# Replacing the framework's instruction order by a kernel's own list schedule, in a fused sparse-attention and feed-forward kernel

## The chip, the cores and the metric

The kernel runs on one core of a Trainium2 chip. The metric is the device time of one execution in microseconds (us), as the median over several runs. Engines are named as the profile names them: PE is TensorE, DVE is VectorE, ACT is ScalarE, POOL is GpSimd, SP is SyncE, whose queue issues most of the DMAs.

## The reference

The reference is attention over selected chunks of 32 keys, followed by a feed-forward layer with a gate.

```python
q, k, v: (4, 8, 768, 64) float32            # batches, heads, positions, head size
k_min, k_max = min and max of k over each chunk of 32 positions
ub    = sum(maximum(q * k_min, q * k_max), -1)       # bound for each (position, chunk)
ub    = where(chunk is not in the future, ub, -1e9)
top   = the 6 chunks with the largest ub
mask  = (the key's chunk is in top) & (key position <= query position)
attn  = softmax(where(mask, q @ k.T / 8, -1e9))
x     = (attn @ v), heads side by side               # 3072 x 512
out   = (relu(x @ w_gate) * (x @ w_val)) @ w_out     # 512 -> 1536 -> 512
```

## The kernel before

The kernel walks through 20 jobs. A job is two heads of one batch; in batch 0 each pair of heads is cut into two jobs of 384 positions, so there are 8 small jobs and then 12 full ones. For each job it loads q, k and v, casts them to bf16 on POOL, transposes q and k, takes minima and maxima of k on DVE, computes bounds and the selection, writes the selection as extra rows of the operand `qx`, computes scores and exponentials, masks the diagonal blocks on POOL, multiplies by v, and transposes the result into `xT`. The feed-forward layer of a batch can start when all four jobs of its positions are done. It has units (a gate group and a value group of four matmuls each, then a relu on ACT and a product on DVE) and output tiles (12 matmuls, a copy on ACT, a store).

In batches 0 and 1 the transposes are done by PE; in batches 2 and 3 the DMA does them. That is so in both kernels.

```python
PE_KQ = PE_SEL = PE_X = lambda b: b < 2

def setup_rest():
    for kx in kx_l:                      # indicator rows: which key lies in which chunk
        for h in range(2):
            g = 64 - 64 * h
            nc.vector.tensor_scalar(out=kx[h][g:g + 64, :]..., in0=ident[...].to_broadcast(...),
                                    scalar1=DROP, scalar2=None, op0=ALU.mult)      # 64x768, eight of them
    # ... cut: memsets

def stage_SELT(j):                       # selection -> rows of qx
    sT = turned(st["sel"][:, ra:r1], r1 - ra, "sel", on_pe)
    eng = (nc.scalar, nc.vector) if on_pe else (nc.vector, nc.vector)
    halves([qx[1][0:64, ts], qx[0][64:128, ts]], sT, eng)
# ... cut: k and q copies in stage_TR choose their engines in the same way

def u_s1(b, nt, u, wide):                # one feed-forward unit
    # ... cut: two PSUM buffers, one each for gate and value (one double one if wide)
    for ps, w in ((g_ps, wg_sb[gi]), (v_ps, wv_sb[gi])):
        for kt in range(KT_):
            nc.tensor.matmul(ps, w[:, kt, cs], xTb[:, kt, x0:x0 + SH], ...)
    nc.scalar.activation(out=grl, in_=g_ps, func=ACT.Relu)
    nc.vector.tensor_tensor(out=hTb[:, nt, :], in0=v_ps, in1=grl, op=ALU.mult)

W_AT = {2: [(w_in, 0)], 4: [(w_in, 1)], 5: [(w_in, 2)], 6: [(w_in, 3)], ...}   # weights, issued by POOL

for s in range(-1, NJ + 2):              # order of recording; the framework's scheduler then
    stage_LD(s + 3); stage_CAST(s + 2)   # orders every engine by its own costs
    stage_UB(s + 1); stage_SELT(s + 1); stage_CASTV(s + 1); weights of W_AT[s + 1]
    stage_TR(s + 2)
    # ... cut: scores of s and attention-times-v of s - 1 alternate, with a quota of units
    stage_XT(s - 1)
```

The softmax here doesn't subtract the row's maximum and nothing guards it: scores larger than these inputs give would overflow.

## Time and profile before

| | before |
|---|---|
| median | 341.52 us (341.18 to 342.4, 4 runs) |
| span of the profiled run | 339.6 us |
| PE busy | 286.9 us (84%) |
| DVE, ACT, POOL busy | 197.9, 168.5, 90.3 us |

PE's busy time contains pipeline fill and half-speed stretches, so I use a second measure. Both kernels issue the same 2344 matmuls. Taking each at its columns / 2.4 GHz + 2.5 ns, and at least 27 ns (the matmuls of 48 columns start 25 to 29 ns apart once PE is at full speed), gives 258.0 us of streaming for the whole program. This is an estimate of the least time that PE needs; "lost" below is the time of a stretch less the streaming of the matmuls that start in it, so it holds idle time and the extra time of matmuls at half speed alike. The Trainium skill ("TensorE: Matmul & The Clock Gate", part 1) gives N / 2.4 GHz plus about 2.5 ns for a warm array: in the tail 22 units of 8 matmuls of 384 columns took 1.32 us each, against 1.30 by the formula. The program before loses 339.6 - 258.0 = 81.6 us.

From the page of the kernel before: busy times, then rows in which each digit is one fortieth of the span (8.5 us) in tenths busy, the granted PE clock, and the DMA engines; at last the small k loads, with the median time from issue to landing.

```profile
PE 286.9 (84%) x2318; PEld 170.7 (50%) x2344; DVE 197.9 (58%) x621; ACT 168.5 (50%) x269; POOL 90.3 (27%) x176
...
PE   1435578999788899987898979998999999999995
...
DVE  8953765888879994688876733354653310343300
...
PEclk9999999999989999997999999999999999999999
DMA  6999999999399794574541232221111023000022
...
k_raw<-in_k_dram SPq DMA_DIRECT2D x16, 96.0 KB, 5.0
```

PE climbs slowly for 60 us. DVE is near full in the first two slices. The DMA engines are full from the second slice to about 85 us.

From PE's list of waits (total us, number, longest us):

```profile
PE v_ps L375 <- DVE hTb L379: 8.9, 12, 2.2
PE o_ps L335 <- POOL aT L316: 6.5, 4, 5.4
```

From POOL's timeline (start, duration, instruction, idle time before it and who ended it):

```profile
10.33 0.91 POOL L411 DMA_DIRECT2D wg_61<-in_moe_w_gate_dram  x1
...
22.35 0.53 POOL L185 CAST vb_81<-v_raw 128x384 bf16<-128x384 f32 x1 [3.20 <-DMA v_raw<-in_v_dram]
26.48 0.51 POOL L180 CAST k_bf<-k_raw 128x384 bf16<-128x384 f32 x1 [3.60 <-DMA k_raw<-in_k_dram]
26.93 0.74 POOL L412 DMA_DIRECT2D wv_67<-in_moe_w_val_dram  x1
27.68 1.12 POOL L316 TENSOR_SCALAR_AFFINE_SELECT aT<-aT 128x256 bf16<-128x256 bf16 x3
```

These lines belong together. The weight DMAs begin at 10.3 us, in front of loads that are needed sooner. The k load of the fourth job is late, so the cast at 26.48 us stands waiting, and behind it in POOL's queue stand the masks of 27.68 us, whose first inputs, ACT's exponentials, were ready at 17.5 us. PE waits 5.4 us for them. The Trainium skill (same page, "Architectural detail", on engine queue depths) calls the queues of ACT and DVE strict FIFO, and GpSimd's strict FIFO for each of its cores; the trace agrees: the masks start at 27.68 us, after the late cast and a weight issue.

Two neighbouring matmuls of 384 columns, from PE's timeline:

```profile
47.61 0.52 PE L375 MATMUL g_ps<-xTb,wg_61 128*128 128x384 bf16 x1
47.93 0.52 PE L375 MATMUL v_ps<-xTb,wv_65 128*128 128x384 bf16 x1
```

They start 0.32 us apart, which is 1.2 GHz. This lasts until 58 us; afterwards such matmuls start 0.16 us apart. The skill's page describes this as the clock gate: an array that is not busy enough runs at half speed. The page's granted clock reads 9 (full) throughout these 58 us, but that is no measurement: the trace's first clock record starts at 58.5 us, and a stretch without a record is shown as full. The later records are full except for two stretches of 3.4 us at half speed, from 92.6 and from 154.1 us.

### The profile page before, as it was taken

The numbers are of one execution on the slowest core, as the hardware profiler recorded it, in microseconds if no ns is written. First come the engines' busy times: TensorE is split into PE (matmuls) and PEld (weight loads), VectorE is DVE, ScalarE is ACT, GpSimd is POOL, SyncE is SP. The second block draws the span as 40 slices with busy tenths as digits, with TensorE's granted clock in tenths as the row PEclk, the third lists the DMA queues.
The fourth block names the chain that finished last, engine by engine and source line by source line (L and its number), as shares of the span: only waits on it lengthen the run. The fifth ranks groups of instructions, "written<-read, shape, count | busy, mean of one in ns | idle before, by whom it ended". The sixth has DMA issues, their size and how long they took to land.

```text
span 339.6 us, 6292 instructions
## 1 busy us (share of the span) xinstructions
PE 286.9 (84%) x2318; PEld 170.7 (50%) x2344; DVE 197.9 (58%) x621; ACT 168.5 (50%) x269; POOL 90.3 (27%) x176
## 2 busy tenths in 40 slices
PE   1435578999788899987898979998999999999995
PEld 0213355566455555554455645464666554555542
DVE  8953765888879994688876733354653310343300
ACT  2472365588775534485355544463656532334221
POOL 3637707332563421274201202030201100000000
PEclk9999999999989999997999999999999999999999
DMA  6999999999399794574541232221111023000022
GB/s 141 176 199 211 216 213 212 219 189 226 74 204 192 141 163 138 151 128 87 55 88 20 46 21 85 83 88 19 25 19 27 0 87 116 31 2 0 2 93 93
DMA packets 108958, 36.32 MB, mean 107 GB/s; under 512 B 100224, under 2 KB 105856, under 8 KB 108928
## 3 DMA queue, kind: packets, MB, share of 16 engines
q1 hardware_dynamic: 103104, 31.21, 45.2%
q0 software_dynamic: 5824, 4.72, 9.1%
q8 instruction: 18, 0.29, 0.4%
q14 instruction: 12, 0.10, 0.1%
HBM read 28.31 MB, written 6.29 MB: 102 GB/s over the span
## 4 chain that ended last, share of the span: by engine, by line
PE 55%; DMA 16%; DVE 15%; ACT 4%; issue 3%; SPq 3%; POOL 2%; POOLq 0%; ACTq 0%; DVEq 0%
PE y_ps L386 17%; PE v_ps L375 9%; PE gv_w L375 9%; PE g_ps L375 8%; PE sT L305 6%; DMA v_raw<-in_v_dram 5%; PE o_ps L335 4%; DMA k_raw<-in_k_dram 4%; DVE hTb L379 3%; SPq L144 3%; DMA sel_tr<-sel_76 3%; DMA k_tr<-k_bf 2%; DVE kmm L221 2%; ACT aT L309 2%; DVE kmm L222 1%
## 5 line engine op out<-in xcount | busy, mean ns | idle before, releaser
L309 ACT ACTIVATE aT<-sT 128x1024 bf16<-128x1024 f32 x96 | 85.0, 919 | 41.0 <-PE sT L305 20.1
L316 POOL TENSOR_SCALAR_AFFINE_SELECT aT<-aT 128x256 bf16<-128x256 bf16 x96 | 39.1, 422 | 111.5 <-ACT aT L309 111.5
L379 DVE TENSOR_TENSOR hTb<-v_ps,grl 128x384 bf16<-128x384 f32 x72 | 39.9, 554 | 30.1 <-PE v_ps L375 15.1
L378 ACT ACTIVATE grl<-g_ps 128x384 bf16<-128x384 f32 x72 | 35.2, 489 | 36.9 <-PE g_ps L375 27.8
L335 PEld LDWEIGHTS <-aT 128*128 128x128 bf16 x672 | 31.6, 102 | 22.2 <-POOL aT L316 7.5
L386 PEld LDWEIGHTS <-hTb 128*128 128x128 bf16 x288 | 27.1, 98 | 30.3
L390 ACT ACTIVATE y_sb<-y_ps 128x512 f32<-128x512 f32 x24 | 14.3, 597 | 48.2 <-PE y_ps L386 45.2
L340 DVE RECIPROCAL zr<-o_ps 128x6 f32<-128x6 f32 (+1 forms) x40 | 7.4, 186 | 39.3 <-PE o_ps L335 38.9
L379 DVE TENSOR_TENSOR hTb<-gv_w,grl 128x384 bf16<-128x384 f32 x24 | 13.4, 558 | 21.8 <-ACT grl L378 21.8
L378 ACT ACTIVATE grl<-gv_w 128x384 bf16<-128x384 f32 x24 | 11.8, 490 | 20.4 <-PE gv_w L375 20.4
L375 PE MATMUL v_ps<-xTb,wv_65 128*128 128x384 bf16 x72 | 17.7, 339 | 2.9 <-DVE hTb L379 2.6
L341 DVE TENSOR_TENSOR x_sb<-o_ps,zr 128x384 bf16<-128x384 f32 (+1 forms) x40 | 19.1, 476 | 1.2
L386 PE MATMUL y_ps<-wo_71,hTb 128*128 128x512 bf16 x72 | 19.5, 379 | 0.1
L386 PE MATMUL y_ps<-wo_72,hTb 128*128 128x512 bf16 x71 | 19.4, 379 | 0.1
L386 PE MATMUL y_ps<-wo_70,hTb 128*128 128x512 bf16 x71 | 19.2, 379 | 0.1
L180 POOL CAST k_bf<-k_raw 128x768 bf16<-128x768 f32 (+1 forms) x20 | 14.4, 720 | 16.8 <-DMA k_raw<-in_k_dram 7.5
L386 PE MATMUL y_ps<-wo_69,hTb 128*128 128x512 bf16 x64 | 18.4, 378 | 0.4
L375 PE MATMUL g_ps<-xTb,wg_61 128*128 128x384 bf16 x72 | 16.8, 338 | 0.7 <-DVE xTb L354 0.6
L375 PE MATMUL v_ps<-xTb,wv_68 128*128 128x384 bf16 x72 | 14.9, 325 | 2.8 <-DVE hTb L379 2.7
L375 PE MATMUL v_ps<-xTb,wv_67 128*128 128x384 bf16 x72 | 14.8, 325 | 2.5 <-DVE hTb L379 2.3
L180 POOL CAST q_bf<-q_raw 128x768 bf16<-128x768 f32 (+1 forms) x20 | 14.3, 714 | 9.1 <-issue 4.9
L375 PE MATMUL v_ps<-xTb,wv_66 128*128 128x384 bf16 x72 | 14.8, 325 | 1.4 <-DVE hTb L379 1.3
(229 smaller groups left out, 541.0 us busy)
## 6 DMA issues: line engine op xcount, KB each, us to landing
out_dram<-y_sb SPq DMA_DIRECT2D x24, 256.0 KB, 2.0
k_raw<-in_k_dram SPq DMA_DIRECT2D x12, 384.0 KB, 5.8
q_raw<-in_q_dram SPq DMA_DIRECT2D x12, 384.0 KB, 6.0
v_raw<-in_v_dram SPq DMA_DIRECT2D x12, 384.0 KB, 4.2
k_raw<-in_k_dram SPq DMA_DIRECT2D x16, 96.0 KB, 5.0
q_raw<-in_q_dram SPq DMA_DIRECT2D x16, 96.0 KB, 5.2
v_raw<-in_v_dram SPq DMA_DIRECT2D x16, 96.0 KB, 5.2
wg_61<-in_moe_w_gate_dram POOLq DMA_DIRECT2D x1, 384.0 KB, 6.6
```

Of the source, the lines that this page charges most:

```text
L144: nc.sync.dma_start(out=t[:, h], in_=s[h].rearrange("(r p) d -> p r d", p=128))
L180: nc.gpsimd.tensor_copy(out=t, in_=st[nm + "r"].rearrange("p h r d -> p r h d"))
L305: nc.tensor.matmul(sT[:, h, o:o + w], kx[h][:, c * 128:(c + 1) * 128], qx[h][:, qb * 128:qb * 128 + w], start=(si == 0), stop=(si == len(b ...
L309: nc.scalar.activation(out=aT[:, :, a0:a0 + o], in_=sT[:, :, 0:o], func=ACT.Exp, scale=scale)
L316: nc.gpsimd.affine_select(out=d, in_=d, compare_op=ALU.is_ge, fill=0.0, base=0, channel_multiplier=-1, pattern=[[0, 2], [1, 128]])
L335: nc.tensor.matmul(o_ps[:, r - r0, :], aT[:, h, o:o + 128], vb[:, h, c, :], start=(p == 0), stop=(p == NP - 1))
L341: nc.vector.tensor_tensor(out=x_sb[:, :, h * D:(h + 1) * D], in0=o_ps[:, :, 0:D], in1=zr.to_broadcast([128, nr, D]), op=ALU.mult)
L375: nc.tensor.matmul(ps, w[:, kt, cs], xTb[:, kt, x0:x0 + SH], start=(kt == 0), stop=(kt == KT_ - 1))
L378: nc.scalar.activation(out=grl, in_=g_ps, func=ACT.Relu)
L379: nc.vector.tensor_tensor(out=hTb[:, nt, :], in0=v_ps, in1=grl, op=ALU.mult)
L386: nc.tensor.matmul(y_ps, hTb[:, nt, tl * 128:(tl + 1) * 128], wo_sb[nt // NPG][:, nt % NPG, :], start=(nt == 0), stop=(nt == NTI - 1))
L390: nc.scalar.activation(out=y_sb, in_=y_ps, func=ACT.Copy)
```

## The change

The intent is to take the order of all five engines away from the framework's scheduler. The kernel describes its work as some 1600 pieces, each with an engine, a cost in us, a priority, its inputs and the buffers that it takes and holds. A small list scheduler plays these forward in time: whenever an engine is free, it takes the ready piece with the lowest priority number. The pieces are then recorded in that order under a manual schedule for all engines. DMA transposes in the last two batches were there before; new among them is only that x is transposed in two halves. The change also divides on-chip buffers anew: loads get three small and two full-size buffers where both sizes shared three, casts get two of each size where both shared two, and the transposed x has four of 384 columns.

```diff
+class Plan:
+    LAG = {"PE": 0.1, "ACT": 0.1, "DVE": 0.1, "POOL": 0.12, "SP": 0.1, "DMA": 1.9, "SDMA": 1.9}
+    def op(self, eng, cost, prio, fn, after=(), makes=(), take=(), hold=(), lag=None): ...
+    def order(self): ...     # list scheduling; hardware-queue DMAs run at 0.27 of their rate
+                             # while weight DMAs are in flight                    (cut)
...
+    def turned(...):         # DMA transposes: the plan lets 2.6 us pass until they land
+            op("SP", 1.25, prio, f, after=after, makes=makes, take=[(tag, name)], hold=hold,
+               lag=2.6)
...                           # indicator rows: halves, on ACT and POOL instead of DVE
+                    op("ACT" if half == 1 or hp < 2 else "POOL", 0.5,
+                       (-90 + hp) if half == 0 else 1.5 + 0.5 * hp, f_ind, ...)
...                           # k, q and selection copies, all batches: one half on ACT, one on DVE
-            if not on_pe:
-                eng = (nc.vector, nc.vector)
+        eng = ("ACT", "DVE")
...                           # feed-forward units: gate and value are two pieces
+        for m, nm in ((0, gn), (1, vn)):
+            op("PE", 0.645, p + 0.001 * m, lambda m=m: f_mm(m), ...)
...                           # output tiles: two pieces of six matmuls
+        cut = NTI // 2
+        for part, (n0, n1) in enumerate(((0, cut), (cut, NTI))): ...
...                           # weights: only after the q load of the fourth job
+        weights(("w", i), [...], (1.0, 4.0, 5.0, 6.0)[i], [("ld", "q", HP - 1)])
...
+    seq = plan.order()
+    with tc.manual_schedule(engines={ENG.PE, ENG.Activation, ENG.DVE, ENG.Pool, ENG.SP}):
+        for i in seq:
+            f = plan.ops[i][3]
+            if f is not None:
+                f()
```

## The prediction

> **What bounds the kernel now.** One core, 341.5 us; TensorE (PE) is busy 286.9 of the 339.6 us span (first part of the page). That flatters it: I summed the matmuls of the timeline at columns/2.4 GHz plus 2.5 ns each and got about 245 us of streaming work. So about 95 us are not streaming. By stretch of the timeline, streamed work against time: 0 to 59.5 us, 16.5 (43 lost); 59.5 to 289 us, 185 (45 lost); 289 to the end, 44 (7 lost).
>
> - Opening: the 16 DMA engines are saturated from 8.5 to 85 us (table of stretches). VectorE is busy 14.9 of the first 17 us, 5.5 of it the eight indicator writes (0.56 to 0.76 us each). GpSimd takes its work in a bad order: its triangular masks sit behind a cast that waits for a k load, and PE waits 5.4 us for them at 22.8 us; a v load costs 10.6 us more at 41 us. PE also runs at half speed: 384-column matmuls start 0.32 us apart until 58 us, 0.16 us after. The Trainium skill ("TensorE: Matmul & The Clock Gate", part 1) says that an idle array falls to 1.2 GHz; the spacing agrees, although the page's granted clock reads full.
> - Middle: a feed-forward unit is two groups of 0.65 us, but often takes 1.7 us, because its two PSUM buffers are freed by the ScalarE relu (0.49) and the VectorE product (0.55). List of waits: PE waits 8.9 us for that product. Around 153 us matmuls are half speed again. Streams are only 5.3 to 6.1 of 8.5 us in 85 to 119, 144 to 170, 195 to 204, 229 to 238.
> - Tail: the last 24 units and 6 output tiles, nearly dense.
>
> **What changes.** Matmul work, PSUM buffers (2+2x2+2 banks) and bytes stay. DMA transposes in the last two batches are already in the old kernel; new there is only that x is transposed in two halves (8 more transposes). The real change is the order on all five engines from a costed list schedule, plus moves: indicator writes from VectorE to ScalarE and GpSimd as halves; in batches 2 and 3 half of the k, q and selection copies from VectorE to ScalarE. Cost: about -5.5 us VectorE in the opening, -12 later (0.4 to 0.6 each), about +24 ScalarE (0.48 at 384, 0.80 at 768 columns), to about 193 us, still not binding. Weights start after the first q and k loads instead of between them. Output tiles come in halves of six matmuls, laced with attention; the last units pair as gate a, gate b, value a, value b.
>
> **On the critical path.** Opening: indicators, masks and order give 6 to 10 us; the DMA floor stays. Middle: better lacing, fewer cold windows: 10 to 18 of 45. Tail: 0 to 2. Sum 16 to 30.
>
> **Predicted: 320 us, 80% range 307 to 333.** Faster by over 2%: 0.89; within 2%: 0.09; slower: 0.02.
>
> **Right if:** PE's idle falls from 53 to about 33 us at equal matmul counts; streamed work by 59.5 us rises from 16.5 to 22 or more; the 5.4 us wait for the masks is gone; the wait for the product falls below 5 us; VectorE falls to about 180, ScalarE rises to about 190; DMA bytes equal.
>
> **Wrong if:** the weights, now later, hold up the first units; fixed orders with wrong costs (half-speed matmuls, queued DMAs) give head-of-line stalls, seen as new waits of 3 us or more; the GpSimd indicator writes delay the first casts; ScalarE's extra copies delay exponentials. Then 335 or more.

## More of the kernel before

A k load of 96 KB takes 5.0 us.

In the middle of the kernel, DVE's and then PE's timeline:

```profile
160.79 0.87 DVE L234 TENSOR_SCALAR qmn<-q_tr 128x768 bf16<-128x768 bf16 x1
161.57 0.35 DVE L239 TENSOR_SCALAR qmx<-q_tr 128x768 bf16<-128x768 bf16 x1
161.84 0.31 DVE L206 COPY qx_2_99<-sel_tr 64x640 bf16<-64x640 bf16 x1
162.16 0.32 DVE L206 COPY qx_2_98<-sel_tr 64x640 bf16<-64x640 bf16 x1
162.52 0.56 DVE L379 TENSOR_TENSOR hTb<-v_ps,grl 128x384 bf16<-128x384 f32 x1
```

```profile
163.13 0.81 PE L375 MATMUL v_ps<-xTb,wv_66 128*128 128x384 bf16 x4 [0.85 <-DVE hTb L379]
```

The product at 162.52 us stands behind four clippings and copies of the next jobs' q and selection. It frees the buffer that PE's next value group needs; PE waits 0.85 us.

## The result, and the profile after

The changed kernel runs in 313.35 us (313.06 to 314.41, 4 runs), against 341.52 us before in the same rounds. The ratio is 0.9177 (95% interval 0.9149 to 0.9206).

The page of the changed kernel, with the same rows (a slice is now 7.8 us):

```profile
PE 278.6 (90%) x2344; PEld 167.9 (54%) x2344; DVE 180.0 (58%) x593; ACT 193.3 (62%) x305; POOL 93.7 (30%) x180
...
PE   0465579998899999999999999999999999999994
...
DVE  2687666878698988787888760345434102432210
...
PEclk9999998999999999999999999999999999999999
DMA  6889999999699999976356112221101131000002
...
kraw<-in_k_dram SPq DMA_DIRECT2D x16, 96.0 KB, 2.5
```

PE's idle time falls from 339.6 - 286.9 = 52.7 us to 311.2 - 278.6 = 32.6 us, and from the seventh slice on PE is nearly full. DVE's load is 18 us lower, ACT's 25 us higher. A 96 KB k load takes 2.5 us, half of before. PE's waits:

```profile
PE kT L321 <- POOL kbf L382: 7.5, 1, 7.5
PE selT L321 <- DVE kx_1_89 L339: 2.8, 2, 2.4
...
PE vl L633 <- DVE hT L652: 0.2, 1, 0.2
```

The wait for the product has shrunk from 8.9 to 0.2 us, and the wait for the masks is gone. A new 7.5 us wait at the start leads the list. POOL's timeline shows both ends:

```profile
5.76 1.16 POOL L307 TENSOR_SCALAR kx_3_93<-ident 64x384 bf16<-64x384 bf16 x1
6.99 0.50 POOL L382 CAST kbf<-kraw 128x384 bf16<-128x384 f32 x1
...
13.17 0.53 POOL L382 CAST kbf<-kraw 128x384 bf16<-128x384 f32 x1 [0.24 <-DMA kraw<-in_k_dram]
17.10 0.81 POOL L539 TENSOR_SCALAR_AFFINE_SELECT aT<-aT 128x256 bf16<-128x256 bf16 x2 [3.41 <-ACT aT L527]
17.86 0.50 POOL L382 CAST qbf<-qraw 128x384 bf16<-128x384 f32 x1
18.31 0.98 POOL L691 DMA_DIRECT2D wg_61<-in_moe_w_gate_dram  x1
```

The first cast now stands behind four indicator writes, so PE's first matmul starts at 7.54 us (4.57 before). But the cast of the fourth job's k is done at 13.7 us, 13 us sooner than before; the masks follow as soon as ACT's exponentials are there; and the first weights are issued at 18.3 us, after those loads.

### The profile page after: what moved, and what is told of

Read it like the earlier page. It is cut to its first block, busy times and chain, and to the rows that moved or that the text cites. A ratio compares the mean times of both kernels' runs of the same rounds, so it can differ in the third digit from the quotient of the medians.

```text
span 311.2 us, 6361 instructions
## 1 busy us (share of the span) xinstructions
PE 278.6 (90%) x2344; PEld 167.9 (54%) x2344; DVE 180.0 (58%) x593; ACT 193.3 (62%) x305; POOL 93.7 (30%) x180
## 3 DMA queue, kind: packets, MB, share of 16 engines
q0 software_dynamic: 5824, 4.72, 9.7%
## 4 chain that ended last, share of the span: by engine, by line
PE 82%; ACT 7%; DVE 6%; issue 2%; POOL 2%; POOLq 0%; ACTq 0%; DVEq 0%
PE g L633 25%; PE yp L669 20%; PE vl L633 15%; PE sT L515 12%; PE o L566 6%; DVE kmm L399 2%; ACT aT L527 2%; PE ub L451 1%; PE kT L321 1%; PE selT L321 1%; PE xt L321 1%; ACT qmx L426 1%; ACT qx_1_96 L337 1%; ACT qx_0_94 L337 1%; ACT kx_1_88 L337 1%
## 5 line engine op out<-in xcount | busy, mean ns | idle before, releaser
L644 ACT ACTIVATE grl<-g 128x384 bf16<-128x384 f32 x96 | 46.5, 489 | 40.9 <-PE g L633 35.9
L652 DVE TENSOR_TENSOR hT<-vl,grl 128x384 bf16<-128x384 f32 x72 | 40.0, 555 | 28.4 <-PE vl L633 23.5
L669 PEld LDWEIGHTS <-hT 128*128 128x128 bf16 x288 | 27.5, 98 | 30.1
L679 ACT ACTIVATE y<-yp 128x512 f32<-128x512 f32 x24 | 14.3, 596 | 36.9 <-PE yp L669 36.8
L399 DVE TENSOR_REDUCE kmm<-kT 128x24 bf16<-128x768 bf16 (+1 forms) x40 | 31.4, 784 | 8.2 <-PE kT L321 4.5
L633 PE MATMUL g<-xT,wg_61 128*128 128x384 bf16 x96 | 19.6, 325 | 0.3 <-DVE xT L599 0.2
L633 PE MATMUL g<-xT,wg_62 128*128 128x384 bf16 x96 | 19.1, 325 | 0.7 <-ACT grl L644 0.6
L669 PE MATMUL yp<-wo_71,hT 128*128 128x512 bf16 x72 | 19.5, 379 | 0.0
L669 PE MATMUL yp<-wo_72,hT 128*128 128x512 bf16 x72 | 19.4, 379 | 0.0
L669 PE MATMUL yp<-wo_69,hT 128*128 128x512 bf16 x72 | 19.4, 379 | 0.0
L669 PE MATMUL yp<-wo_70,hT 128*128 128x512 bf16 x72 | 19.4, 379 | 0.0
L581 DVE TENSOR_TENSOR x<-o,zr 128x384 bf16<-128x384 f32 (+1 forms) x40 | 18.8, 472 | 0.6
L633 PE MATMUL g<-xT,wg_63 128*128 128x384 bf16 x96 | 18.9, 325 | 0.0
L633 PE MATMUL g<-xT,wg_64 128*128 128x384 bf16 x96 | 18.9, 326 | 0.0
L382 POOL CAST kbf<-kraw 128x768 bf16<-128x768 f32 (+1 forms) x20 | 13.9, 699 | 9.2 <-DMA kT<-kbf 7.2
L382 POOL CAST qbf<-qraw 128x768 bf16<-128x768 f32 (+1 forms) x20 | 13.9, 698 | 5.7 <-issue 2.3
L633 PE MATMUL vl<-xT,wv_68 128*128 128x384 bf16 x72 | 14.5, 325 | 1.0 <-ACT grl L644 1.0
```

Source lines behind the costliest of these rows:

```text
L382: nc.gpsimd.tensor_copy(out=t, in_=TL[rn].rearrange("p h r d -> p r h d"))
L399: nc.vector.tensor_reduce(out=TL[mm][:, m, c0:c1], in_=kT().rearrange("f (c t) -> f c t", t=CH), axis=AX.X, op=o)
L581: nc.vector.tensor_tensor(out=TL[xn][:, :, h * D:(h + 1) * D], in0=TL[on][:, :, 0:D], in1=TL[zn].to_broadcast([128, nr, D]), op=ALU.mult)
L633: nc.tensor.matmul(ps, w[:, kt, cs], TL[xn][:, kt, :], start=(kt == 0), stop=(kt == KT_ - 1))
L644: nc.scalar.activation(out=new("grl", rn), in_=g, func=ACT.Relu)
L652: nc.vector.tensor_tensor(out=TL[hn][:, nt, :], in0=vv, in1=TL[rn], op=ALU.mult)
```

## The experiments

Every run gave a correct result. The table gives median, ratio to the old kernel and interval, and the lost time (as defined above) by stretch of the profiled run. The trace of the old kernel lacks 26 matmul records, all of 512 columns and after 80 us, worth 5.7 us of streaming, so its lost times by stretch add up to 87.3 instead of 81.6 (the last two are too high); those of all others are complete. The changed kernel's own ratio comes from other rounds than those of the experiments, so differences under about half a per cent mean nothing here.

| run | median us | ratio (95%) | lost 0 to 59.5 | lost 59.5 to 153 | lost 153 to end |
|---|---|---|---|---|---|
| before | 341.5 | 1 | 45.0 | 18.5 | 23.8 |
| changed | 313.4 | 0.918 (0.915 to 0.921) | 38.1 | 7.2 | 8.0 |
| before_moves | 338.9 | 0.991 (0.984 to 0.999) | 42.8 | 15.8 | 20.1 |
| order_only | 317.5 | 0.929 (0.922 to 0.935) | 40.9 | 7.7 | 8.2 |
| tile_order | 332.4 | 0.973 (0.966 to 0.979) | 45.7 | 11.4 | 13.6 |
| no_dma_lag | 316.1 | 0.925 (0.920 to 0.930) | 38.3 | 8.9 | 8.9 |
| pool_free | 329.0 | 0.961 (0.955 to 0.967) | 49.8 | 9.9 | 8.1 |
| pe_free | 312.7 | 0.913 (0.906 to 0.919) | 39.5 | 7.7 | 6.6 |
| vec_free | 327.0 | 0.957 (0.949 to 0.964) | 36.6 | 15.7 | 13.5 |
| flat_costs | 363.0 | 1.063 (1.054 to 1.071) | 51.1 | 24.0 | 26.9 |
| weights_early | 323.7 | 0.944 (0.941 to 0.948) | 38.6 | 15.8 | 8.5 |
| whole_groups | 324.7 | 0.949 (0.945 to 0.953) | 39.6 | 17.0 | 10.1 |
| ind_act | 315.6 | 0.922 (0.918 to 0.926) | 36.4 | 10.3 | 8.1 |
| ind_pool2 | 313.1 | 0.914 (0.910 to 0.918) | 37.5 | 8.1 | 7.9 |

### Moves or order? (before_moves, order_only)

The change bundles moved work and a new order. These two runs complete a square of four: moves without the order, and the order without the moves.

```diff
 # before_moves: the kernel before, with the moves
-nc.vector.tensor_scalar(out=<64x768 of kx>, in0=<ident>, scalar1=DROP, ...)
+<the same in two halves, on nc.scalar, or nc.gpsimd for the first half of hp 2 and 3>
-eng = (nc.scalar, nc.vector) if on_pe else (nc.vector, nc.vector)     # k, q
+eng = (nc.scalar, nc.vector)
-eng = (nc.scalar, nc.vector) if on_pe else (nc.vector, nc.vector)     # selection
+eng = (nc.vector, nc.scalar)
```

> The kernel before, with only the moves of the change: indicator writes in halves on ScalarE and GpSimd, half of the k, q and selection copies of batches 2 and 3 on ScalarE; the order is still the framework's. Theory A (the order made the gain: with VectorE's in-order queue no longer standing behind copies that wait for DMA transposes): 332 to 342 us. Theory B (the moves made it by relieving VectorE): 316 to 325 us.

Measured: 338.88 us, ratio 0.991.

```diff
 # order_only: the changed kernel, moves undone, planned anew
-op("ACT" if half == 1 or hp < 2 else "POOL", 0.5, ...)      # 16 half indicator writes
+op("DVE", 0.7, -1.95 + 0.3 * hp, ...)                       # 8 whole ones
+if not on_pe: eng = ("DVE", "DVE")                          # k, q and selection copies
```

> The changed kernel with the moves undone: whole indicator writes on VectorE, all batch 2 and 3 copies on VectorE, the list schedule made anew for this. Theory A: 311 to 320 us, the gain stays. Theory B: 328 us or more. VectorE busy should be back at about 198 us and ScalarE at about 169 in either.

Measured: 317.49 us, ratio 0.929. DVE was busy 197.3 us and ACT 170.9, as expected. The moves alone gave 0.9% and the order alone 7.1%; both together gave 8.2%. So the new order, together with the finer pieces that order_only keeps, is the cause, and relieving DVE is a small part. Theory B falls.

### The framework's order on the same pieces (tile_order)

```diff
-    with tc.manual_schedule(engines={ENG.PE, ENG.Activation, ENG.DVE, ENG.Pool, ENG.SP}):
-        for i in seq: ...
+    for i in seq: ...
```

> The changed kernel, its pieces recorded in the planned sequence, but without the manual schedule, so that the framework's scheduler orders the engines again. If the order on the engines is the cause, it gives back most of the gain, 325 us or more; if it is the cut of the work into smaller pieces, the moves and the sequence of recording, 312 to 318 us.

Measured: 332.42 us, ratio 0.973. Two thirds of the gain are gone, although pieces, moves, buffers and sequence of recording are unchanged. PE's list of waits in this run has the masks back, with the same longest wait as before the change:

```profile
PE o L566 <- POOL aT L539: 11.9, 4, 5.4
```

### Which engine's order? (pool_free, pe_free, vec_free)

The manual schedule can be given for some engines only. In each of these runs the orders of the engines that were not freed are, instruction for instruction, those of the changed kernel.

```diff
-engines={ENG.PE, ENG.Activation, ENG.DVE, ENG.Pool, ENG.SP}
+engines={ENG.PE, ENG.Activation, ENG.DVE, ENG.SP}            # pool_free
+engines={ENG.Activation, ENG.DVE, ENG.Pool, ENG.SP}          # pe_free
+engines={ENG.PE, ENG.Pool, ENG.SP}                           # vec_free
```

> The changed kernel with the order of GpSimd alone given back to the framework's scheduler; the orders of the other four engines are as in the changed kernel. Freeing all five took 332.4 us, 19 us more than the changed kernel, with PE waiting 11.9 us for triangular masks. Theory A1 (GpSimd's order, masks behind casts and weight issues that wait for loads, is the main cost): 5.4 us waits for the masks come back and 319 to 326 us. Theory A2 (PE's or VectorE's order is): within 1% of 313.4 us.

Measured: 328.96 us, ratio 0.961: somewhat more than expected, and nearly all of it is lost by 102 us (13.9 us of streaming behind the changed kernel there). Up to 59.5 us PE streamed 9.7 us of work, against 21.4 in the changed kernel. POOL's timeline and PE's wait:

```profile
10.96 0.97 POOL L691 DMA_DIRECT2D wg<-in_moe_w_gate_dram  x1
...
26.72 0.51 POOL L382 CAST qbf<-qraw 128x384 bf16<-128x384 f32 x1 [2.43 <-DMA qraw<-in_q_dram]
27.18 0.77 POOL L539 TENSOR_SCALAR_AFFINE_SELECT aT<-aT 128x256 bf16<-128x256 bf16 x2
...
51.27 0.50 POOL L373 CAST vb<-vraw 128x384 bf16<-128x384 f32 x1 [12.12 <-DMA vraw<-in_v_dram]
```

```profile
PE o L566 <- POOL aT L539: 16.2, 4, 7.1
```

It is the picture of the old kernel: weights from 11 us, masks behind a cast that waits for a load, and a v cast that blocks the queue for 12.1 us until 51 us.

> The changed kernel with PE's order alone given back to the framework's scheduler. Theory A2 (PE's sequence of ready groups is what matters): 319 us or more. Theory A1: 313 to 316 us.

Measured: 312.67 us, ratio 0.913, so no loss. The test is weaker than it looks. Position by position, with buffer numbers left out, only 222 of the 2344 matmuls in the two traces differ (in tile_order, too, only 313): the framework still gets the pieces in the planned sequence of recording. What it shows is that this much freedom on PE costs nothing once the engines that feed PE keep their planned order; what the old order of PE would cost was not run.

> The changed kernel with the orders of VectorE and ScalarE given back to the framework's scheduler, PE, GpSimd and the DMA queue as in the changed kernel. I expect waits of VectorE for DMA transposes as in the run with all five freed (11.6 us there) and 318 to 325 us; if these orders do not matter, within 1% of 313.4 us.

Measured: 327.03 us, ratio 0.957, 2 us above the expected range. Here the opening is untouched (36.6 us lost) and the loss lies after 59.5 us. DVE's timeline at the longest wait, and the list of its waits for DMA:

```profile
130.69 0.56 DVE L581 TENSOR_TENSOR x<-o,zr 128x384 bf16<-128x384 f32 x1
134.64 0.32 DVE L339 COPY qx<-selT 64x640 bf16<-64x640 bf16 x1 [3.39 <-DMA selT<-sel]
```

```profile
DVE qx L339 <- DMA selT<-sel: 8.9, 7, 3.4
...
DVE kmm L399 <- DMA kT<-kbf: 3.8, 4, 1.8
```

DVE reached a copy of the transposed selection 3.39 us before that had landed, and everything behind it stood still. So the gain of the opening depends on POOL's order and the gain of the middle on DVE's and ACT's (these two were not freed one by one, and SP's order not by itself). The two losses (15.6 and 13.7 us) add up to more than the 19.1 us of freeing all five. An explanation that no run isolates: with all engines freed, PE's order adapts to the late operands, while in pool_free and vec_free it stays fixed.

### Is it the waiting for DMA transposes? (no_dma_lag)

My first theory of the middle was that the plan knows when a transpose lands.

```diff
-               lag=2.6)      # both kinds of DMA transpose
+               lag=0.1)
```

> The changed kernel with one constant of the plan changed: the time that the plan allows for a DMA transpose to land, 2.6 us, set to 0.1, so that the plan puts the copies of transposed k, q and selection (and what reads x) too early in the in-order queues. Theory A expects new waits of VectorE and ScalarE for the transposes' landing of 1 to 2.5 us each, some 24 of them, and 318 to 326 us. If waits for transposes did not matter in the middle of the kernel: within 1% of 313.4 us.

Measured: 316.07 us, ratio 0.925. The waits came back, and they cost little. DVE's list of waits:

```profile
DVE qx L339 <- DMA selT<-sel: 7.6, 6, 2.3
```

In this run DVE waits 7.6 us for transposed selections, and ACT another 4.3 us; the changed kernel has none of it. The time rose by 2.7 us, below the expected 318 to 326 and within the 1% that was to mean that these waits do not matter. vec_free has 13.0 us of such waits on DVE and 6.2 on ACT and costs 13.7 us. So theory A in its narrow form, copies waiting for transposes, explains only a small part. DVE's and ACT's orders matter as a whole.

### What the plan must know (flat_costs, whole_groups)

```diff
+        if eng in ("PE", "ACT", "DVE", "POOL"):
+            cost = 0.5                             # flat_costs
```

> The changed kernel with a plan that knows no durations for PE, VectorE, ScalarE and GpSimd: every piece costs 0.5 us in the plan; DMA costs, lags, priorities and buffer limits are kept. If the measured costs carry the gain: 325 us or more. If priorities, readiness and buffer limits carry it: 313 to 320 us.

Measured: 363.03 us, ratio 1.063. With the same dependences, priorities and buffer limits, but no durations, the plan is 6% slower than the framework's order. From PE's list of waits:

```profile
PE o L568 <- POOL aT L541: 16.8, 5, 7.7
PE kT L323 <- POOL kbf L384: 15.0, 3, 7.5
PE g L635 <- ACT grl L646: 12.0, 23, 0.7
```

The engines then meet pieces whose inputs are not there yet, and the loss is spread over all stretches. One flat value was tried; how coarse the costs may be was not.

```diff
-        for m, nm in ((0, gn), (1, vn)): op("PE", 0.645, ...)      # whole_groups
+        op("PE", 1.29, p, lambda: (f_mm(0), f_mm(1)), ..., take=[("F", gn), ("F", vn)])
-        for part, (n0, n1) in enumerate(((0, cut), (cut, NTI))):
+        for part, (n0, n1) in enumerate(((0, NTI),)):
-            for part, (x0, x1) in enumerate(((0, cut), (cut, NP))):
+            for part, (x0, x1) in enumerate(((0, NP),)):
 # (and the plan's test of a free buffer made right for a piece that takes two)
```

> The changed kernel with the finer pieces undone: gate and value groups are one piece of 1.29 us, output tiles one piece of 12 matmuls, attention-times-v one piece a head; the plan is made anew. If the finer cut with its gate-gate-value-value pairs matters: 320 to 328 us. If not: 312 to 317 us.

Measured: 324.68 us, ratio 0.949. The loss is nearly all between 59.5 and 204 us, where attention and units share PE. In the tail, 255 us to the end, this kernel loses 4.2 us against the changed kernel's 6.7, so the gate-gate-value-value pairs there gave nothing. A piece is the smallest thing that the plan can place: coarse pieces, with the plan made anew for them, cost 11 us.

### When the weights start (weights_early)

In pool_free both the masks and the weight issues moved, since POOL issues the weights too. This run moves the weights' start alone, but the plan is made anew around it, so that other orders move too: position by position 1044 of 2344 matmuls and 360 of DVE's 593 instructions differ from the changed kernel.

```diff
-                ..., [("ld", "q", HP - 1)])        # after the q load of the fourth job
+                ..., [("ld", "q", 1)])             # after that of the second
```

> The changed kernel with one edge of the plan changed: the weights may be issued once the q load of the second piece of work has landed, not the fourth, about 8 us sooner, as in the kernel before; the plan is made anew around it. If the weights' early bytes, which starve the k and q loads, caused the opening's loss in the run with GpSimd's order freed: 319 to 328 us, streamed work by 59.5 us down to 12 or less from 21.4. If the place of the masks behind blocked casts caused it: 312 to 316 us, since the plan places the masks well around any weights.

Measured: 323.66 us, ratio 0.944. The time is as the theory of starved loads had it, but the place is not: by 59.5 us PE had streamed 20.9 us of work, not 12 or less. The loss is between 59.5 and 153 us. The small k loads on the page, and POOL's casts of the loads of batch 0:

```profile
kraw<-in_k_dram SPq DMA_DIRECT2D x16, 96.0 KB, 5.3
```

```profile
9.22 0.97 POOL L691 DMA_DIRECT2D wg<-in_moe_w_gate_dram  x1
...
40.50 0.51 POOL L382 CAST kbf<-kraw 128x384 bf16<-128x384 f32 x1 [4.42 <-DMA kraw<-in_k_dram]
...
52.92 0.51 POOL L373 CAST vb<-vraw 128x384 bf16<-128x384 f32 x1 [2.05 <-DMA vraw<-in_v_dram]
```

The weights start at 9.2 us; the small k loads take 5.3 us, about as in the old kernel; batch 0's last v cast stands at 52.9 us, and PE transposes the sixth job's x at 77.1 us, against 66.4 us in the changed kernel. The feed-forward layer starts sooner (43.7 us against 50.2) and then runs out of work. The Trainium skill ("DMA: Bandwidth & Descriptors", "Issuing engines are not separate DMA queues") says that DMAs of all queues run on the same 16 engines and interleave; the doubling of the small k loads' time shows what that costs here. How much of the 10 us is this, and how much the other orders of the new plan, no run separates. pool_free's further 5.3 us, and its empty opening, remain for the place of the casts and masks in POOL's queue; that is a difference of two runs, and was not run by itself. The traces support it: in weights_early PE's list has no wait for masks at all, with the weights as early, while in pool_free it has 16.2 us.

### The new wait at the start (ind_act, ind_pool2)

The plan costs the POOL indicator writes at 0.5 us; they take 1.16 to 1.19 us, and PE waits 7.5 us for the first cast. Two runs tried to win that time; in both the plan is made anew (982 of 2344 matmuls stand elsewhere in ind_act, 103 in ind_pool2).

```diff
-op("ACT" if half == 1 or hp < 2 else "POOL", 0.5, (-90 + hp) if half == 0 else ...)
+op("ACT", 0.5, (-90 + hp if hp < 2 else -1.95 + 0.3 * hp) if half == 0 else ...)      # ind_act
+op(<as before>, 0.5 or 1.2 on POOL, (-90 + hp if hp < 2 else 0.2 * hp) if half == 0 else ...)   # ind_pool2
```

> The changed kernel with the four GpSimd indicator writes (1.16 to 1.19 us each on the chip, 0.5 in the plan) moved to ScalarE, after its own first four. They made PE wait 7.5 us for the first k cast. If the late start is on the critical path: 309.5 to 312 us, first matmul at about 4.6 us. If the DMA and VectorE pace the opening anyway: 312.5 to 314.5 us.

Measured: 315.63 us, ratio 0.922. PE's first wait did shrink:

```profile
PE kT L321 <- POOL kbf L382: 4.7, 1, 4.7
```

> The changed kernel with the GpSimd indicator writes kept, but costed at 1.2 us in the plan as measured and with a priority behind the first casts, so that two stand before them and two between later casts. First matmul at about 5 us. If the late start is on the critical path: 310 to 312.5 us; else 312.5 to 314.5 us.

Measured: 313.14 us, ratio 0.914. PE's first matmul started at 4.72 and 5.09 us instead of 7.54, and neither run is faster than the changed kernel beyond the noise; ind_act lies above both of its expected ranges, ind_pool2 in the one that says the late start is not on the critical path. In ind_act the opening lost 1.7 us less and the next stretch 3.1 us more. So ind_pool2, the nearer of the two to the changed kernel, says that the longest single wait of PE in the new profile is not on the path that sets the time. No run here beats the changed kernel clearly.

## Why the prediction was right, point by point

- **Total.** 320 us was predicted, 307 to 333 as range; 313.35 was measured. The gain was 28.2 us instead of 21.5.
- **Opening, "6 to 10" us.** By 59.5 us the lost time fell from 45.0 to 38.1 us, so 6.9. The streamed work by then is 21.4 us, just short of the 22 that the prediction asked for, though from a lower start. (The prediction's 16.5 us of streamed work was too high: it took runs of unequal matmuls as equal; record by record it is 14.5. Hence also its total of 245 us instead of 258, so that the program before loses 82 us and not 95.)
- **Reasons for the opening.** The masks and their wait were named rightly: the 5.4 us wait went, and freeing POOL's order brought 16.2 us of such waits back. The indicator writes were over-rated: with all other moves they take 2.2 us off the opening's lost time in the old kernel (before_moves) and 2.8 us under the new order (changed against order_only), and an earlier first matmul gave nothing. The failure named for them, that they delay the first casts, did come, as a new wait of 7.5 us, and did not cost what was feared. The later start of the weights stood in the prediction as a risk; weights_early puts it at about 10 us, the plan made anew included.
- **Middle, "10 to 18 of 45".** This is the term that was mis-sized. From 59.5 us on, the old kernel loses 81.6 - 45.0 = 36.6 us and the changed one 15.2, so the middle and tail gave 21.4 us, with nothing from the tail. The prediction had counted the opening's and the middle's decisions as separate. They are not: starting the weights early, with the plan made anew, costs its time after 59.5 us (15.8 us lost up to 153 us, against 7.2). And DVE's and ACT's order, by vec_free, is worth 13.7 us by itself.
- **"Better lacing" on PE.** Right in one part and not shown in the other. Finer pieces, which are what PE can lace, are worth 11 us (whole_groups); PE's own order within them cost nothing when it was given back, in the weak test of pe_free. The wait for the product fell from 8.9 to 0.2 us because DVE reached the products in time: it is 0.6 us in order_only, where DVE has all its old copies back, and 3.7 us in vec_free.
- **Moves off DVE, "-5.5" and "-12" us.** DVE fell by 17.9 us and ACT rose by 24.8, as predicted, and it was worth about 1%.
- **"Fixed orders with wrong costs".** The risk was real: flat costs gave 363 us. The plan's costs were good enough where it mattered, and wrong by a factor of two where it did not (POOL's indicator writes).
- **Half speed.** The spacing of PE's matmuls shows half speed until 58 us before, and with an interruption until 49 us after. It was not tested by itself, but the clock records bound it. Matmuls worth 16.1 us of streaming start in stretches at half speed before and 10.8 us after, and each takes about as long again, so by this estimate PE saves some 5 of the 28 us directly; the two later stretches, from 92.6 and 154.1 us, are gone. The main cause it is not: before_moves has 8.8 us at half speed, less than the changed kernel, and takes 25.5 us longer.

## What to carry to other kernels

In-order queues make the order of the feeding engines a resource: look at what stands behind an instruction that waits, above all on an engine that is mostly idle, as POOL is here (30% busy in the changed kernel, and 15.6 us lost when its order alone is taken back, the earlier weight issues included). Here a schedule of one's own needed durations: the same scheduler with flat costs was 6% slower than the framework's. Small pieces added to it: with coarse ones it was still 5% faster than the old kernel, against 8%. Bulk transfers that are needed late are worth holding back until the small loads that are needed first are through, even if the DMA engines stay busy either way; pool_free and weights_early, each with something else changed too, both point that way.

## What the Trainium skill lacked or had wrong

- "TensorE: Matmul & The Clock Gate", part 1, gives a sustained busy window of about 3.4 us for the way to full speed, but not which share of busy time counts as busy. Here matmuls ran at half speed (384 columns every 0.32 us) through slices in which PE was busy 4.9 to 6.9 of 8.5 us (34 to 59.5 us). The page warns that recorded clock events can be unreliable; those on record fit the spacing (in the changed kernel matmuls of 128 columns go from 0.107 to 0.056 us apart at 42.5 us, where the first record starts), but there is none before the first change to full speed, which a profile page then shows as full.
- "GPSIMD Engine Reference", section 4.1, calls one-input elementwise work on GpSimd roughly line-rate. A multiply by a constant of a broadcast 64x384 bf16 took 1.16 to 1.19 us there (spans on that engine are rough in this profile); a cast of 128x384 took 0.50 us on the same engine; and VectorE did the same multiply at 64x768, twice the size, in 0.56 to 0.76 us.
- "DMA: Bandwidth & Descriptors" says that queues interleave on the same engines, but not what a stream of casting weight loads costs small loads beside it: 96 KB loads took 2.5 to 2.6 us in the median in the changed kernel (first weights at 18.3 us), 5.0 to 5.2 us in the kernel before (10.3 us), and 3.5 to 5.3 us in weights_early and pool_free (9.2 and 11.0 us).
- No page has a figure for what head-of-line blocking in the strict FIFO queues costs: here 15.6 us of 313 for GpSimd's order (with the early weights) and 13.7 us for VectorE's and ScalarE's.
